# First halves of all heads ahead of second halves in every batch, stacks of two head pairs in the raw weights' room, and the exponential's scale and bias from one VectorE instruction

## The chip, the cores and the metric

The kernel runs on one core of a Trainium2 chip. The metric is the device time of one execution in microseconds, median of several runs. Five engines work side by side, each through its own list of instructions in order: TensorE (PE, with its weight loads listed as PEld), VectorE (DVE), ScalarE (ACT), GpSimd (POOL) and SyncE (SP), which here only issues DMAs.

## What is computed

Four batches of eight attention heads (768 positions, 64 wide) with a hash mask, then a two-layer network over the 3072 tokens:

```
q_bucket, k_bucket = 6 sign bits of q @ proj, k @ proj
scores = where(q_bucket == k_bucket, q @ k.T / 8, -1e9)
attn   = softmax(scores);  x = attn @ v          # x: 3072 x 512
out    = relu(x @ w_in)**2 @ w_out               # w_in 512 x 2048, w_out 2048 x 512
```

## The kernel before, in words

**Units and visits.** Heads are taken in pairs (four pairs, `hp`, to a batch `b`). A visit `(b, hp, half)` handles 384 of the 768 query rows for both heads of a pair: six units of 128 rows, three for each head (`unit`, L720). There are 32 visits and 192 units, numbered from 0 in the code and from 1 in the text. A unit computes 128 x 768 scores in PSUM (`pS`), a row maximum on DVE (the tile `line`), the exponential on ACT (`e`), and then in the later visits two float16 halves of the divided rows (`hl`, ACT and DVE), which one DMA transposes into `aT`. In early "plain" visits (`PLAIN_AV`) the rows stay float32, GpSimd divides them, TensorE transposes them (`pT`) and ACT or DVE copies them to `aT`. `av` (L764) multiplies `aT` with the values into `pA` and splits the result into `xx`.

**Scores and stacks.** In batch 0 the scores are one float32 product of two stacked operands (tiles `A`, `Q`, `L`, `M`; a matmul `pS<-A,L` or `pS<-Q,M`). In batches 1 to 3 they are two float16 products of four stacked operands (`A`, `Q`, `L`, `M`, each half a tile). `prep` (L627) makes a pair's stacks: it loads the pair (`R<-kq`), computes the sign bits (`pd`, `bits`) and their masks (`pc`), in batches 1 to 3 also power-of-two scales (`bounded`, L596), and sends pieces between partitions by DMA. Each of the four tile names has two buffers, so the stacks of two pairs live at a time.

**Weights.** `fetch` (L517) loads a 128 x 512 piece of a weight matrix (`raw`, two buffers), rebuilds float32 values in `f` (seven buffers, helper tiles `top`), and `split` writes two float16 halves to `win` or `wo`. There are 32 such pieces.

**The network.** When all four pairs of a (batch, half) are done, one of eight stages of `moe` (L787) may start. A stage has 16 steps of 12 matmuls `pm<-xx,win` (384 columns) and 9 matmuls `po<-wo,g` (512 columns). The first stage uses `wo` as converted; `align` (L574) then rescales the 16 slices of `wo` for the other stages (`move` at L584, on ACT, DVE or POOL).

**What sets the order.** All instructions are recorded first (`Program.add`), then a planner (`order`, L244) gives each engine its list, from prices per instruction (`cost`), ranks, and `PACE` (L65), which ties the network's 896 groups of three matmuls to units: a group may not start before its unit's scores. `WHOLE = {0: 2}` and L880 set the visits: in batch 0 pairs 0 and 1 whole, then the first halves of pairs 2 and 3, then their second halves; in batches 1 to 3 every pair whole. So in batches 1 to 3 the first half's stage becomes possible one visit before the second half's. `ALTERNATE = 36` (L723) lets every other of the first 36 units put its scores into the PSUM room of `po`; later units share the single `pS`.

**The lines of a unit that change.** After the maximum, two tiny DVE instructions make the scale and the bias that the exponential reads:

```
todo = [("tensor_reduce", (nmx, sS, AX.XY, ALU.max), {"negate": True})]
if len(st) > 1:
    todo += [("tensor_scalar", (scale, nmx, MASK * MASK / 2, factor[st[1][0].rec], ALU.is_lt, ALU.mult), {}),
             ("tensor_scalar", (bias, nmx, scale, 1.0, ALU.mult, ALU.mult), {})]
```

Of the kernel before, what the change touches and what calls it, by code (L numbers as in the profile page):

```python
# [33 lines left out]
MASK = 49152.0  # L34
ASC = float(2.0**14)


BUFS = dict(xx=12, hl=3, raw=2, f=7, e=3, aT=3, g=2, A=2, Q=2, L=2, M=2, RV=2, VV=6)
# [14 lines left out]
PLAIN, PLAIN_TO, ALTERNATE = 4, 8, 36  # L53

PLAIN_AV, DIVIDE = (0, 1, 2, 4, 5), ("pool",)
# [3 lines left out]
WHOLE = {0: 2}  # L59
# [5 lines left out]
PACE = ((25, 0), (64, 120), (193, 680))  # L65
# [58 lines left out]
class Program:  # L124
# [12 lines left out]
    def tile(self, pool, kind, shape, dtype, name, bufs=1, tag=None):  # L137
        line = self.tags.setdefault((id(pool), tag or name), [])
        make = lambda: pool.tile(shape, dtype, name=name, tag=tag or name, bufs=bufs)
        rec = Buffer(kind, int(np.prod(shape[1:])), line[-bufs] if len(line) >= bufs else None, make)  # L140
        line.append(rec)
        rec.line, rec.bufs = line, bufs
        self.n += 1
        return View(rec, self.shadow.dram_tensor(f"{name}_{self.n}", shape, dtype, kind="Internal").ap(), ())

    @staticmethod
    def region(view):
        ap, rec = view.ap, view.rec
        size = lambda dims: 1 + sum(st * (n - 1) for st, n in dims)
        if rec.kind == "dram":  # L150
            return 0, 1, ap.offset, ap.offset + size(ap.ap), 0, 0, 0
        p0, f0 = divmod(ap.offset, rec.row)
        if rec.kind == "psum":
            return 0, 1, 0, 1, 0, 0, 0

        (step, n), inner = ap.ap[1], size(ap.ap[2:])
        block = (step, f0 % step, f0 % step + inner) if n > 1 and f0 % step + inner <= step else (0, 0, 0)
        return (p0, p0 + ap.ap[0][1], f0, f0 + size(ap.ap[1:])) + block
# [32 lines left out]
    def cost(key, name, args, kw):  # L191
# [3 lines left out]
        if name == "chain":  # L195
            t = sum(Program.cost(key, *x)[0] for x in args)
            return t, t
# [245 lines left out]
def lsh_attention_moe(ctx: ExitStack, tc, kq, v, proj2, w_in, w_out, consts, out):  # L443
# [44 lines left out]
    sgn_f = sb([P, 4 * P], F32, "sgn_f", tag="o")  # L488
# [23 lines left out]
    tops = [sb([P, 512, 2], F16, f"top{n}") for n in range(2)]  # L512
    for x in tops:
        dve.memset(x.bitcast(F32), 0.0)
    turn = [0]

    def fetch(src):  # L517

        raw = sb([P, 512, 2], U32, "raw", BUFS["raw"])
# [4 lines left out]
        f = sb([P, 512], F32, "f")  # L524
        dve.scalar_tensor_tensor(f.bitcast(U32), raw[:, :, 0], 13, first.rearrange("p n t -> p (n t)").bitcast(U32), ALU.logical_shift_right, ALU.bitwise_or)
        return f
# [47 lines left out]
    def align():  # L574
# [17 lines left out]
    halved, factor = [], {}  # L592
# [3 lines left out]
    def bounded(Rs):  # L596
# [17 lines left out]
        both = sb([P, 8], F32, "both")  # L614
        size, flip = both[:, 0:4], both[:, 4:8]
        dve.tensor_scalar(size, pn, 2.0**8, 2.0**120, ALU.max, ALU.min)
        dve.tensor_scalar(u32(size), u32(size), 1, 0x7F800000, ALU.logical_shift_right, ALU.bitwise_and)
        dve.tensor_scalar(u32(flip), u32(size), 0x7F800000, 0x7F800000, ALU.bitwise_xor, ALU.bitwise_and)
        found = sb([P, 4], F32, "found", 4)
        own, exact = found[:, 0:2], found[:, 2:4]  # L620
        for n, h in enumerate((T, U)):
            dve.tensor_scalar(own[h], flip[h, 2 * n : 2 * n + 2], 2.0**-51, 1.0, ALU.mult, ALU.mult)
        dve.tensor_scalar(size, size, 2.0**50, 1.0, ALU.mult, ALU.mult)
        dve.scalar_tensor_tensor(exact, size[:, 0:2], SC, size[:, 2:4], ALU.mult, ALU.mult)
        return own, exact

    def prep(b, hp, plain):  # L627
# [19 lines left out]
        if not plain:  # L647
            own, exact = bounded(Rs)
        out = []
        for odd, R in enumerate(Rs):  # L650
# [3 lines left out]
            else:  # L654

                A, Q, L, M = [x[:, n] for x in (sb([P, 2, S], F16, name) for name in ("AL", "QM")[odd]) for n in range(2)]
# [19 lines left out]
            else:  # L676
# [3 lines left out]
                factor[M.rec] = exact[:, odd : odd + 1]  # L680
# [4 lines left out]
    def scale_values(b):  # L685
# [3 lines left out]
        for hp in range(H // 2):  # L689
# [30 lines left out]
    def unit(st, half, i, aT, plain):  # L720
# [9 lines left out]
        line = sb([P, 3], F32, "line", 2)  # L730
        nmx, bias, scale = [line[:, n : n + 1] for n in range(3)]
        todo = [("tensor_reduce", (nmx, sS, AX.XY, ALU.max), {"negate": True})]
        if len(st) > 1:
            todo += [("tensor_scalar", (scale, nmx, MASK * MASK / 2, factor[st[1][0].rec], ALU.is_lt, ALU.mult), {}),
                     ("tensor_scalar", (bias, nmx, scale, 1.0, ALU.mult, ALU.mult), {})]
# [3 lines left out]
        to = {"bias": bias, "scale": scale} if len(st) > 1 else {"bias": nmx}  # L739
# [47 lines left out]
    def moe(n, b, half):  # L787
# [5 lines left out]
        for f in range(NF + 1):  # L793
# [21 lines left out]
            if f > 0:  # L815
# [17 lines left out]
                if n == 0 and m == 3:  # L833
                    acc = sb([P, 3, DM], F32, "acc")
                for t in range(3):
# [8 lines left out]
                    elif last:  # L844
                        o = sb([P, DM], F32, "o", tag="f")

# [31 lines left out]
    for b in range(B):  # L878
        F = WHOLE.get(b, H // 2)
        visits += [(b, hp, half) for hp in range(F) for half in range(2)] + [(b, hp, 0) for hp in range(F, H // 2)] + [(b, hp, 1) for hp in reversed(range(F, H // 2))]  # L880
# [72 lines left out]
```

## Time and profile before

| What | Value |
|---|---|
| Median of 3 runs | 904.04 us (901.77 to 905.07) |
| The profiled execution's own time | 904.71 us |
| Its span, first to last instruction | 902.9 us |
| Mean granted TensorE clock | 0.994 |
| PE busy | 850.8 us, 94% |
| DVE busy | 685.0 us, 76% |
| ACT busy | 666.7 us, 74% |
| POOL busy | 107.7 us, 12% |
| DMA queue of SP, share of 16 engines | 62.1% |

The profile shows one execution. Busy times are sums over the span; a stage of the kernel is looked at through windows of the span. The row maximum of unit 24 starts at 81.1 us, of unit 36 at 126.9, unit 48 at 185.3, unit 72 at 285.5 and unit 192 at 769.8; the stages below are cut just behind the 24th, 72nd and 192nd.

### The profile page before, as it was taken

How to read it: one execution, taken by the hardware profiler on the slowest of the kernel's cores; microseconds unless marked ns; L12 is line 12 of the kernel's file. 1: busy time of each engine (PE TensorE's matmuls, PEld its weight loads, DVE VectorE, ACT ScalarE, POOL GpSimd, SP SyncE). 2: the span in 40 equal slices, each digit the busy share in tenths (PEclk: the TensorE clock that was granted, in tenths of full speed). 3: DMA queues.
4: the chain of work that ended last, by engine and by line, in shares of the span. 5: the costliest groups of instructions: out<-in, count | busy, mean ns of one | idle time of the engine just before them, and what ended most of it. 6: DMA issues, size and time to landing. Idle time of an engine off the chain costs nothing. (4 is left out here: it accounts for less than half of the span.)

```text
span 902.9 us, 14665 instructions
## 1 busy us (share of the span) xinstructions
PE 850.8 (94%) x5095; PEld 449.6 (50%) x5095; DVE 685.0 (76%) x1563; ACT 666.7 (74%) x1217; POOL 107.7 (12%) x158
## 2 busy tenths in 40 slices
PE   8997989998888999799999999999999999999997
PEld 6553544554444555445454555544445555555553
DVE  5899889999999888888888888898879876211111
ACT  4875777998789988888879887888779766533433
POOL 1665554100200000000000000000000000000000
PEclk9998999999999999999999999999999999999999
DMA  7447637689878676868879776777757736400000
GB/s 246 138 152 199 198 111 210 134 169 193 177 157 158 141 139 133 180 131 170 167 124 204 120 150 103 170 148 119 156 112 167 123 53 116 77 1 1 35 1 36
DMA packets 279978, 120.06 MB, mean 133 GB/s; under 512 B 258272, under 2 KB 266080, under 8 KB 279904
## 3 DMA queue, kind: packets, MB, share of 16 engines
q1 hardware_dynamic: 279424, 119.11, 62.1%
q8 instruction: 40, 0.66, 0.3%
q14 instruction: 34, 0.28, 0.1%
q10 hardware_dynamic: 480, 0.01, 0.0%
HBM read 37.30 MB, written 6.29 MB: 48 GB/s over the span
## 5 line engine op out<-in xcount | busy, mean ns | idle before, releaser
L430 PE MATMUL po<-wo,g 128*128 128x512 f16 x1152 | 324.4, 379 | 3.6 <-DVE g L430 1.5
L430 PE MATMUL pm<-xx,win 128*128 128x384 f16 x1536 | 322.6, 326 | 3.9 <-ACT g L430 2.8
L430 ACT ACTIVATE e<-pS,line 128x768 f32<-128x768 f32 x192 | 185.7, 967 | 65.1 <-DVE line L428 56.0
L430 PEld LDWEIGHTS <-win 128*128 128x128 f16 x1536 | 149.3, 98 | 117.1 <-issue 10.8
L428 DVE TENSOR_REDUCE line<-pS 128x1 f32<-128x768 f32 x192 | 182.7, 952 | 29.6 <-PE pS L430 27.7
L430 PEld LDWEIGHTS <-g 128*128 128x128 f16 x1152 | 110.7, 98 | 131.2 <-issue 11.8
L430 DVE SCALAR_TENSOR_TENSOR hl<-e,rv,hl 128x768 f16<-128x768 f32 x162 | 165.4, 1023 | 9.9 <-ACT hl L430 9.7
L430 ACT ACTIVATE hl<-e,rv 128x768 f16<-128x768 f32 x157 | 145.8, 930 | 30.7 <-ACT e L430 15.2
L430 DVE SCALAR_TENSOR_TENSOR g<-g,g 128x384 f16<-128x384 f32 x118 | 65.6, 556 | 107.7 <-ACT g L430 106.2
L430 ACT ACTIVATE g<-g 128x384 f32<-128x384 f32 (+1 forms) x242 | 125.1, 519 | 5.1 <-PE po L430 0.4
L430 ACT ACTIVATE g<-pm 128x384 f32<-128x384 f32 x128 | 61.8, 483 | 76.2 <-PE pm L430 75.8
L423 PE MATMUL pA<-aT,VV 128*64 128x384 f16 x972 | 87.8, 328 | 0.0
L430 POOL TENSOR_SCALAR rv<-sm 128x1 f32<-128x1 f32 x69 | 26.3, 381 | 484.3 <-ACT e L430 483.3
L423 PEld LDWEIGHTS <-VV 128*64 128x64 f16 x972 | 51.1, 110 | 36.3 <-issue 16.2
L430 PE MATMUL pS<-A 128*128 128x384 f16 x144 | 35.0, 324 | 12.4 <-ACT e L430 11.9
L430 PE MATMUL pS<-Q 128*128 128x384 f16 x144 | 35.8, 325 | 7.9 <-ACT e L430 7.3
L430 PE MATMUL pS<-A,L 128*128 128x384 f32 x96 | 39.7, 529 | 2.8 <-ACT e L430 2.7
L430 PE MATMUL pS<-Q,M 128*128 128x384 f32 x96 | 37.0, 502 | 2.9 <-ACT e L430 2.1
L430 DVE TENSOR_SCALAR rv<-sm 128x1 f32<-128x1 f32 x123 | 18.4, 150 | 25.9 <-ACT e L430 25.7
L430 ACT ACTIVATION_READ_ACCUMULATOR e<-pS,line 128x1 f32 x192 | 37.7, 196 | 0.0
L430 PE MATMUL pS<-M 128*128 128x384 f16 x144 | 35.4, 325 | 0.0
L430 PE MATMUL pS<-L 128*128 128x384 f16 x144 | 35.3, 325 | 0.0
(130 smaller groups left out, 844.2 us busy)
## 6 DMA issues: line engine op xcount, KB each, us to landing
R<-kq SPq DMA_DIRECT2D x24, 384.0 KB
raw<-w_in SPq DMA_DIRECT2D x16, 511.8 KB
raw<-w_out SPq DMA_DIRECT2D x16, 511.8 KB
V<-vp SPq DMA_DIRECT2D x16, 384.0 KB
out<-o SPq DMA_DIRECT2D x21, 256.0 KB
aT<-hl SPq DMA_TRANSPOSE x162
A<-A SPq DMA_DIRECT2D x24, 96.0 KB
Q<-Q SPq DMA_DIRECT2D x24, 96.0 KB
```

What stands on the lines that cost most here:

```text
L423: ins = q.engine.matmul(*map(real, args), **kw).ins
L428: issue(q, getattr(q.engine, name)(*map(real, args), **{k: real(x) for k, x in kw.items()}).ins)
L430: ins = getattr(q.engine, o.name)(*map(real, o.args), **{k: real(x) for k, x in o.kw.items()}).ins
```

## The change

What it does:

- `WHOLE` is 0 for every batch: four first halves (pairs 0 to 3), then four second halves, in batches 1 to 3 in the same order of pairs, in batch 0 in reverse. A first half's stage of the network becomes possible after half of a batch.
- One tile `room` of 26,624 bytes per partition takes the place of `raw`, `top` and `f`. In batches 1 to 3, pairs 2 and 3 put their stacks there; pairs 0 and 1 keep the two buffers of `A`, `Q`, `L`, `M`. So four pairs' stacks live through such a batch. In batch 0 they do not: two pairs are made a second time for their second halves (16 executions of `prep` become 18).
- Plain visits are 0 to 3 in place of 0, 1, 2, 4, 5; `PACE` starts at unit 12 and reaches group 800 at the end in place of 680; `ALTERNATE` falls from 36 to 24.
- `bounded` scales one head's two operands so that the product needs no factor. `unit` then makes scale and bias at once, as a `[P, 2]` result of one `scalar_tensor_tensor` on a line that holds 1.0 and the negated maximum.
- `align` is bound to POOL. Outputs use `acc` in place of buffers of `f`. The planner's price of a chain has 120 ns more per link.

```
-WHOLE = {0: 2}
+WHOLE = {0: 0, 1: 0, 2: 0, 3: 0}
-PACE = ((25, 0), (64, 120), (193, 680))
+PACE = ((12, 0), (36, 60), (193, 800))
-PLAIN, PLAIN_TO, ALTERNATE = 4, 8, 36
+PLAIN, PLAIN_TO, ALTERNATE = 4, 8, 24
-PLAIN_AV, DIVIDE = (0, 1, 2, 4, 5), ("pool",)
+PLAIN_AV, DIVIDE = (0, 1, 2, 3), ("pool",)
+ALIGN_ON = ("pool",)
...
+    room = sb([P, ROOM // 4], F32, "room")
+    place = lambda at, size, dtype: room[:, at // 4 : (at + size) // 4].bitcast(dtype)
...
-            move(x, x, rel[:, n // 4 : n // 4 + 1])
+            move(x, x, rel[:, n // 4 : n // 4 + 1], engines=tuple(getattr(pr, k) for k in ALIGN_ON))
...
+                if b and hp >= 2:
+                    A, Q, L, M = [place(12288 * (hp - 2) + 6144 * odd + 1536 * n, 1536, F16) for n in range(4)]
+                else:
...
-            todo += [("tensor_scalar", (scale, nmx, MASK * MASK / 2, factor[st[1][0].rec], ALU.is_lt, ALU.mult), {}),
-                     ("tensor_scalar", (bias, nmx, scale, 1.0, ALU.mult, ALU.mult), {})]
+            pair = sb([P, 2], F32, "pair", 2)
+            todo += [("scalar_tensor_tensor", (pair, nmx.broadcast_to([P, 2]), MASK * MASK / 2, line, ALU.is_lt, ALU.mult), {})]
+            to = {"scale": pair[:, 0:1], "bias": pair[:, 1:2]}
...
-    for b ... + [(b, hp, 1) for hp in reversed(range(F, H // 2))]
+    for b ... + [(b, hp, 1) for hp in (reversed(range(F, H // 2)) if F or not b else range(H // 2))]
```

The order of the built programs gives, on TensorE, these counts of matmuls up to the scores of a unit (before / after):

| Up to | pm | po | pA f16 | pA f32 | pT | pd | pc |
|---|---|---|---|---|---|---|---|
| unit 24 | 0 / 0 | 0 / 0 | 0 / 0 | 36 / 36 | 108 / 123 | 12 / 16 | 8 / 16 |
| unit 72 | 240 / 349 | 160 / 248 | 216 / 252 | 60 / 48 | 180 / 144 | 32 / 44 | 30 / 41 |
| unit 192 | 1164 / 1308 | 864 / 971 | 936 / 960 | 60 / 48 | 180 / 144 | 64 / 72 | 64 / 72 |
| the end | 1536 / 1536 | 1152 / 1152 | 972 / 1008 | 60 / 48 | 180 / 144 | 64 / 72 | 64 / 72 |

On TensorE before, between the scores of units 31 and 36, the list holds float32 scores and transposes, with single matmuls `pt` of the weights' norms:

```order
L430 MATMUL pS_1339<-A,L 128x384
L430 MATMUL pT<-unit_f,e 128x128 x4
L430 MATMUL pS_1339<-A,L 128x384
L430 MATMUL pT<-unit_f,e 128x128 x2
L430 MATMUL pS<-A,L 128x384
L430 MATMUL pT<-unit_f,e 128x128 x3
```

and in the changed kernel, at the same units, the scores stand between the network's matmuls:

```order
L434 LDWEIGHTS win
L434 MATMUL pm<-xx,win 128x384
L434 MATMUL pS<-A,L 128x384 x2
L434 LDWEIGHTS win
L434 MATMUL pm<-xx,win 128x384
```

The first stage of the network has moved from units 37 and on to units 25 and on, and the plain transposes of these units are gone.

On VectorE before, a unit near the 100th has the maximum, the two tiny instructions, and then other work:

```order
L428 TENSOR_REDUCE line<-pS 128x1
L428 TENSOR_SCALAR line<-line,found 128x1
L428 TENSOR_SCALAR line<-line 128x1
L430 SCALAR_TENSOR_TENSOR hl<-e,rv,hl 128x768
L430 SCALAR_TENSOR_TENSOR g<-g_4823,g 128x384
```

and now, at the same place:

```order
L432 TENSOR_REDUCE line_74<-pS 128x1
L432 SCALAR_TENSOR_TENSOR pair<-line_74 128x2
L434 SCALAR_TENSOR_TENSOR hl<-e,rv,hl 128x768
L434 SCALAR_TENSOR_TENSOR g<-g_5059,g 128x384
```

One instruction has gone from between the maximum and what follows.

On GpSimd before, three slices of `wo` were rescaled there (eight were on ACT, five on DVE):

```order
L430 TENSOR_SCALAR rv<-sm 128x1
L430 TENSOR_SCALAR wo<-wo,rel 128x2x512 x3
L430 TENSOR_SCALAR rv<-sm 128x1 x5
```

and now all sixteen are:

```order
L434 TENSOR_SCALAR wo<-wo,rel 128x2x512 x2
L434 TENSOR_SCALAR rv<-sm 128x1
L434 TENSOR_SCALAR wo<-wo,rel 128x2x512 x4
L434 TENSOR_SCALAR rv<-sm 128x1
L434 TENSOR_SCALAR wo<-wo,rel 128x2x512 x10
```

Thirteen rescalings have moved to GpSimd's list, some of the unit's `rv` behind them. VectorE's last conversion of a weight piece stands at unit 36 now, at unit 48 before.

More of the change, by code (lines that the diff above doesn't have):

```diff
@@ L139, in tile @@
         make = lambda: pool.tile(shape, dtype, name=name, tag=tag or name, bufs=bufs)
-        rec = Buffer(kind, int(np.prod(shape[1:])), line[-bufs] if len(line) >= bufs else None, make)
+        rec = Buffer(kind, int(np.prod(shape[1:])) * mybir.dt.size(dtype), line[-bufs] if len(line) >= bufs else None, make)
         line.append(rec)
@@ L151, in region @@
             return 0, 1, ap.offset, ap.offset + size(ap.ap), 0, 0, 0
-        p0, f0 = divmod(ap.offset, rec.row)
         if rec.kind == "psum":
             return 0, 1, 0, 1, 0, 0, 0
-        (step, n), inner = ap.ap[1], size(ap.ap[2:])
-        block = (step, f0 % step, f0 % step + inner) if n > 1 and f0 % step + inner <= step else (0, 0, 0)
-        return (p0, p0 + ap.ap[0][1], f0, f0 + size(ap.ap[1:])) + block
+        k = mybir.dt.size(view.dtype)
+        p0, f0 = divmod(ap.offset * k, rec.row)
+        (step, n), inner = ap.ap[1], size(ap.ap[2:]) * k
+        step *= k
+        block = (step, f0 % step, f0 % step + inner) if n > 1 and step and f0 % step + inner <= step else (0, 0, 0)
+        return (p0, p0 + ap.ap[0][1], f0, f0 + (size(ap.ap[1:]) - 1) * k + k) + block
     def add(self, *ways):
@@ L195, in cost @@
         if name == "chain":
-            t = sum(Program.cost(key, *x)[0] for x in args)
+            t = sum(Program.cost(key, *x)[0] for x in args) + 120 * (len(args) - 1)
             return t, t
@@ L511, in lsh_attention_moe @@
     wo = sb([P, 2, NF, DM], F16, "wo")
[L512 removed]
+    room = sb([P, ROOM // 4], F32, "room")
+    place = lambda at, size, dtype: room[:, at // 4 : (at + size) // 4].bitcast(dtype)
+    tops = [place(8192 + 2048 * n, 2048, F16).rearrange("p (n t) -> p n t", t=2) for n in range(2)]
     for x in tops:
[L514 to L515 removed]
+        dve.memset(x.rearrange("p n t -> p (n t)").bitcast(F32), 0.0)
+    turn, turned = [0], [0]
     def fetch(src):
[L519 removed]
+        raw = place(turn[0] % 2 * 4096, 4096, U32).rearrange("p (n t) -> p n t", t=2)
         send(raw.rearrange("p n t -> p (n t)").bitcast(U16)[:, 0:2047], src.bitcast(U16)[:, 1:2048])
@@ L590, in matmuls @@
         pr.add((pe, "matmuls", [(a, {"start": start, "stop": stop}) for a in args], {}))
-    halved, factor = [], {}
+    halved = []
+    lines = [sb([P, 2], F32, f"line{n}") for n in range(2)]
+    for x in lines:
+        dve.memset(x, 1.0)
     few = sb([P, 4], BF16, "few")
@@ L647, in prep @@
         if not plain:
-            own, exact = bounded(Rs)
+            own = bounded(Rs)
         out = []
@@ L688, in scale_values @@
         tops = sb([P, H // 2], F32, "vtop", 2)
-        for hp in range(H // 2):
+        for hp in range(H // 2) if b else reversed(range(H // 2)):
             pr.rank = r0 + LOADS * hp
@@ L832, in moe @@
                     back = unscaled(b, m // 4)
-                if n == 0 and m == 3:
+                if last and (n or m == 3):
                     acc = sb([P, 3, DM], F32, "acc")
@@ L879, in lsh_attention_moe @@
         F = WHOLE.get(b, H // 2)
-        visits += [(b, hp, half) for hp in range(F) for half in range(2)] + [(b, hp, 0) for hp in range(F, H // 2)] + [(b, hp, 1) for hp in reversed(range(F, H // 2))]
+        visits += [(b, hp, half) for hp in range(F) for half in range(2)] + [(b, hp, 0) for hp in range(F, H // 2)] + [(b, hp, 1) for hp in (reversed(range(F, H // 2)) if F or not b else range(H // 2))]
     kept, kept_v = {}, {}
```

42 lines of the change are left out of this document (23 added, 19 removed).

## Prediction

> **What bounds the kernel now.** First the page's busy shares:
>
> ```profile
> span 902.9 us, 14665 instructions
> PE 850.8 (94%) x5095; PEld 449.6 (50%) x5095; DVE 685.0 (76%) x1563; ACT 666.7 (74%) x1217; POOL 107.7 (12%) x158
> ```
>
> TensorE is idle for 52 us only. If the change takes no matmul away, it can win little more than these 52 us. Where they lie is read from windows, cut behind the 24th, 36th, 48th, 72nd and 192nd row maximum (columns: width, then busy time of PE, PEld, DVE, ACT, POOL, granted clock, DMA share, GB/s):
>
> ```profile
> 0.00:82.10 82.10, 75.81 (x449) 45.59 (x450) 66.87 (x144) 54.83 (x115) 42.05 (x57) 1.00 0.59 180
> 82.10:126.90 44.80, 37.03 (x179) 19.83 (x179) 39.58 (x84) 30.86 (x61) 21.21 (x31) 0.89 0.58 176
> 126.90:185.30 58.40, 54.43 (x283) 28.18 (x282) 54.98 (x121) 49.25 (x93) 21.25 (x29) 1.00 0.69 166
> 185.30:286.50 101.20, 89.08 (x563) 46.06 (x562) 96.37 (x228) 87.79 (x150) 9.76 (x14) 1.00 0.85 168
> 286.50:770.80 484.30, 468.72 (x2938) 244.47 (x2937) 405.54 (x951) 390.79 (x698) 13.39 (x28) 1.00 0.73 140
> 770.80:902.90 132.10, 125.72 (x691) 65.41 (x688) 21.68 (x40) 53.17 (x104) 0.00 (x0) 1.00 0.07 22
> ```
>
> ```profile
> L428 DVE TENSOR_REDUCE line<-pS x192: 930/951/960, 15.7 to 769.8; 128x1 f32<-128x768 f32 x192
> ```
>
> The last row gives the maxima's first and last start. I call row one of the windows stage 1, rows two to four together stage 2 (units 25 to 72, 204.4 us), row five stage 3, row six stage 4. PE's idle time is 6.3, 23.9, 15.6 and 6.4 us. In stage 2 PE works 180.5 us and DVE 190.9 of the 204.4: there VectorE is the bound (weights are converted, and the first units with float16 stacks begin), and TensorE lacks work that it could do. In stage 3 PE is busy 97%, DVE 84%, ACT 81%. Stage 4 is the network alone.
>
> What TensorE and the row's chain wait for, over the span:
>
> ```profile
> ACT e L430 <- DVE line L428: 56.0, 71, 2.5
> ...
> PE pS L430 <- ACT e L430: 24.1, 31, 2.8
> ```
>
> From unit 37 on there is one score buffer, so the next scores wait for the exponential, and that waits for `line`. Inside, on DVE:
>
> ```profile
> 190.59 0.94 DVE L428 TENSOR_REDUCE line<-pS 128x1 f32<-128x768 f32 x1
> 191.57 0.21 DVE L428 TENSOR_SCALAR line<-line,found 128x1 f32<-128x1 f32 x1
> 191.82 0.21 DVE L428 TENSOR_SCALAR line<-line 128x1 f32<-128x1 f32 x1
> 191.95 1.01 DVE L430 SCALAR_TENSOR_TENSOR hl<-e,rv,hl 128x768 f16<-128x768 f32 x1
> ```
>
> Each dependent link costs 0.25 us (191.82 less 191.57), which is more than its 0.21.
>
> **Part 1: matmuls moved.** Prices come from the chain of waits in stage 4 and from the groups by shape:
>
> ```profile
> 777.35 0.86 PE po L430 x4
> 778.22 1.14 PE pm L430 x7
> 781.25 0.86 PE po L430 x4
> ```
>
> ```profile
> L423 PE MATMUL pA<-aT,VV 128*64 128x384 f16 x972 | 87.8, 328 | 0.0
> ...
> L430 DVE SCALAR_TENSOR_TENSOR g<-g,g 128x384 f16<-128x384 f32 x118 | 65.6, 556 | 107.7 <-ACT g L430 106.2 <-PE pn L430 0.5
> ...
> L430 PE MATMUL pT<-unit_f,e 128*128 128x128 f32 x180 | 27.4, 276 | 2.2 <-ACT aT L430 1.3 <-POOL e L430 0.5 <-DVE cst L430 0.4
> ...
> L430 PE MATMUL pc<-bits,sgn 128*128 128x384 bf16 x64 | 21.3, 333 | 8.6 <-DVE L L430 4.7 <-DVE M L430 2.5 <-DVE norm L430 0.9
> ...
> L423 PE MATMUL pA<-aT,V 128*64 128x384 f32 x120 | 20.5, 490 | 0.3 <-ACT aT L430 0.3
> ...
> L423 PE MATMUL pd<-R,pj 128*32 128x384 f32 x96 | 10.7, 498 | 0.0
> ```
>
> A step of the network (12 `pm`, 9 `po`) takes 3.90 us (781.25 less 777.35); by columns that is 0.162 us a `pm` and 0.216 a `po`. The others, busy over count: `pA` 0.090, `pT` 0.152, `pc` 0.33, and, with two records to a float32 matmul, `pA` f32 0.34 and `pd` 0.22.
>
> With the counts of the change section, up to unit 24: 15 `pT` 2.3, 4 `pd` 0.9, 8 `pc` 2.7: +5.9 us. Up to unit 72: 109 `pm` 17.7, 88 `po` 19.0, 36 `pA` 3.3, 12 `pA` f32 -4.1, 36 `pT` -5.5, 12 `pd` 2.7, 11 `pc` 3.7: +36.8. Up to unit 192: 144 `pm` 23.3, 107 `po` 23.1, 24 `pA` 2.2, -4.1, -5.5, 8 `pd` 1.8, 8 `pc` 2.7: +43.5. At the end: 3.3 - 4.1 - 5.5 + 1.8 + 2.7 = -1.8. So TensorE's work by stage becomes 75.8 + 5.9 = 81.7; 180.5 + 30.9 = 211.4; 468.7 + 6.7 = 475.4; 125.7 - 45.3 = 80.4; together 848.9, as much as before. The gain can come only from idle time, 31 us of work having gone into the stage where PE had 24 us to spare. The second making of two pairs is in these sums; of the other three batches none is made again, since `bounded` stands twelve times in both orders.
>
> **Part 2: VectorE and ScalarE.** In stage 2 DVE gets 9 more `hl` (float16 visits from unit 25 on; 1.01 us each, row in part 3), 9.2 us; 7 more of the network's `g`, 3.9; one more `bounded`, and in each of its five there six more tiny instructions of at most a link, 0 to 7.5, taken as 4. It loses 24 links of 0.25, 6 us, and five rescalings of 0.48, 2.4. That is about +9: 200 us of work. ACT gets nine more `hl` of 0.93 and the moved network's squares and loses eight rescalings of 1.15; I take it as 168 to 178. In stage 3 DVE loses 120 links, 30 us, and gets 7 x 6 x 0.25 = 10 back in `bounded`: 386 us.
>
> The price of the new instruction is not in the trace. The two old ones take 0.38 us together until the next one starts (191.95 less 191.57); the one new one takes at least the second's 0.13 and at most the 0.38, where nothing is saved. I take 0.13, as it differs from the second old one only in being twice as wide. If nothing is saved, DVE has 206 and 416 us, still under PE; I price that at 4 us, the part of the idle time that the shorter chain is to win in stage 3. The rest of the shortening lies under PE's work, since PE waited for the exponential only 31 times.
>
> DMA: six more transposes, two more plain pairs loaded, all by unit 72, where the engines' share was 0.85 at most. SP's list is in order, and what is queued behind them are weight loads and the next stacks. I take nothing for it, and up to 3 us if a load comes late. Writing stacks into `room` waits for the last conversion. That stands at unit 36 on DVE, and the first scores from `room` are unit 61's, 24 units later: hidden.
>
> **Part 3: `align` on POOL.** The rows of the rescalings and of `hl`, with shortest, median and longest time:
>
> ```profile
> L430 ACT ACTIVATE wo<-wo,rel x8: 1137/1150/1157, 258.9 to 273.6; 128x1024 f16<-128x1024 f16 x8
> L430 DVE TENSOR_SCALAR wo<-wo,rel x5: 469/477/479, 262.1 to 268.1; 128x1024 f16<-128x1024 f16 x5
> ...
> L430 POOL TENSOR_SCALAR wo<-wo,rel x3: 1117/1118/1817, 245.0 to 247.1; 128x1024 f16<-128x1024 f16 x3
> ```
>
> ```profile
> L430 DVE SCALAR_TENSOR_TENSOR hl<-e,rv,hl x162: 998/1009/1584, 74.0 to 775.3; 128x768 f16<-128x768 f32 x162
> L430 SPq DMA_TRANSPOSE aT<-hl x162: 1273/1439/2463, 75.1 to 776.4; - x162
> L430 ACT ACTIVATE hl<-e,rv x157: 917/934/949, 76.0 to 774.4; 128x768 f16<-128x768 f32 x157
> ```
>
> Sixteen take 16 x 1.12 = 18 us on POOL, or 29 at the longest. A slice is needed every 3.90 us of the next stage, so POOL keeps ahead; behind it wait only some `rv`, which can also stand on DVE. It takes 2.4 us from DVE and 9.2 from ACT. The longest POOL row is 0.70 us over its median, the longest `hl` 0.58 over its own: two engines seem to get into each other's way at times, and I set that at 2 us, within the idle time below. The Trainium skill ("SBUF — State Buffer", section "Who interferes with whom") says that a VectorE instruction with two SBUF inputs and a GpSimd instruction that reads SBUF exclude each other for a whole instruction; the two longest rows agree, and by that rule the thirteen moved slices speak against the change.
>
> **The clock.** One stretch of stage 2:
>
> ```profile
> 85.00:90.00 5.00, 2.99 (x6) 1.56 (x6) 4.77 (x11) 2.09 (x3) 1.74 (x3) 0.50 0.64 171
> ```
>
> Here PE starved and ran at half speed. With the network's matmuls beside units 25 and on, such a hole closes; The 2.99 us at half speed are 1.5 us of work; I count 0 for it, and 1.5 us at the low end. The Trainium skill ("TensorE: Matmul & The Clock Gate", Part 1) puts the halved clock down to an idle window and lifts it after a few microseconds of work; by that rule the 1.5 us would be won in full, 885.5 in place of 887.
>
> **The sum.** Stage 1: 81.7 + 6.3 idle = 88.0. Stage 2: 211.4 + 12 = 223.4; the 12 are chosen, between 7 (stage 3's share of idle time, 3.2%) and the old 23.9, nearer to stage 3, because PE is now the longest there (211 against 200), but three engines are over 80%. Stage 3: 475.4 + 12 = 487.4, of 15.6 about a quarter won by the shorter chain. Stage 4: 80.4 + 6.4 = 86.8; in the order 36 `pm` and 29 `po`, 12 us, stand behind the last scores ahead of the last `pA`. Before, the last maximum began at 769.8 and the last transpose was issued at 776.4 and took 1.4 us, so 8 us go by there, and 4 are left for its landing; if it lands later, each microsecond counts. Span 885.6; the profiled execution took 1.8 us more than its span (904.71 and 902.9), so 887.4, put at 887, against 904.71 of that execution and a median of 904.04. About 0.5% can be told from no change: under 899.5 is faster, over 908.6 slower.
>
> **Rivals.**
>
> *The idle time stays.* Stage 2 keeps 23.9 and stage 3 15.6, since DVE, ACT and PE all near their limits wait for each other: 887 + 11.9 + 3.6 = 902.5. For it: in the last part of stage 2 before, PE lost 12.1 of 101.2 us although the network was there. Against it: DVE was then 95% busy, and will be 90% (200 of 223.4). Chance 0.13.
>
> *The single score buffer binds, slower.* From unit 25 on there is one `pS`, twelve units earlier, while DVE still converts weights. If each of units 25 to 48 finds one more DVE instruction of `hl`'s 1.01 us ahead of its maximum, PE, in order, stands 24 x 1.01 = 24 us: 911. It decides when the units' period passes what PE has to do, 223.4 / 48 = 4.65 us. For it: units 25 to 36 had two buffers and DVE was busy 39.58 of 44.80. Against it: units 37 to 48 had one, at 4.87 us each, and PE was 93% busy. Chance 0.15.
>
> *GpSimd and VectorE in each other's way.* Thirteen POOL rescalings each hold DVE up for 0.58 to 1.12 us, on the path: 7.5 to 14.6 us, 894 to 902, middle 898. Against it: one of three POOL rows only was long. Chance 0.05.
>
> *Nearly all idle time goes.* Stage 2 at 7, stage 3 at 5 (1%), the clock's 1.5: 887 - 5 - 7 - 1.5 = 873.5. Chance 0.07.
>
> **How the numbers follow.** The forecast has the remaining 0.60. Faster: 0.60 + 0.07 + 0.05 = 0.72; same 0.13; slower 0.15. The range goes from 870, under the best case, to 906, over the rival in which idle time stays; the slower one is left out.
>
> **What would show it.** Right: the 72nd maximum near 310 us (88.0 + 223.4), PE at 94% or more in units 25 to 72, one link of 0.2 to 0.3 us behind each maximum, some 87 us behind the last. Wrong: `PE pS <- ACT e` grown over 24 us and units 25 to 48 longer than 4.65 us each (slower rival); long POOL and `hl` rows during the rescalings (the two in each other's way); PE idle as before in stage 2.

## The result, and the profile after

The changed kernel takes 892.49 us (median of 4 runs, 891.39 to 893.71), the kernel before 904.26 (4 runs, 901.77 to 905.07): a ratio of 0.9875, interval 0.9851 to 0.9898, or 11.8 us less. The profiled execution took 893.71 us, with a granted clock of 0.988 over the span.

The page's busy shares of the changed kernel:

```profile
span 891.9 us, 14603 instructions
PE 845.0 (95%) x5079; PEld 448.0 (50%) x5083; DVE 671.6 (75%) x1482; ACT 670.3 (75%) x1223; POOL 114.8 (13%) x153
```

TensorE's idle time is 46.9 us (891.9 less 845.0), where it was 52.1. Windows of the changed kernel, cut behind the 24th, 72nd and 192nd maximum (columns as before: width, busy PE, PEld, DVE, ACT, POOL, clock, DMA share, GB/s):

```profile
0.00:88.70 88.70, 79.90 (x470) 48.00 (x475) 72.14 (x161) 62.15 (x127) 45.05 (x65) 1.00 0.56 174
88.70:330.60 241.90, 215.77 (x1199) 108.32 (x1198) 205.47 (x440) 181.21 (x324) 62.64 (x71) 0.96 0.72 163
330.60:805.50 474.90, 469.35 (x2964) 250.22 (x2963) 379.02 (x855) 393.10 (x707) 7.13 (x17) 1.00 0.74 141
805.50:891.90 86.40, 80.01 (x452) 41.47 (x449) 15.00 (x28) 33.88 (x66) 0.00 (x0) 0.98 0.12 33
```

The width of a row less its PE time is the idle time: 8.8, 26.1, 5.5 and 6.4 us, against 6.3, 23.9, 15.6 and 6.4 before. One start time given ahead of the prediction is wrong: in the kernel before, the 24th maximum starts at 81.98 us (81.1 is the 23rd), so the cut at 82.1 lies inside it. Cut behind it, stage 2 of the kernel before is 203.5 us long with 23.0 us of idle time, and stage 1 has 7.1:

```profile
82.95:286.50 203.55, 180.54 (x1021) 94.08 (x1021) 190.08 (x429) 167.10 (x302) 52.21 (x73) 0.97 0.74 169
```

So stage 2 kept its idle time and has 3 us more; stage 3 lost two thirds of its own. The waits of the changed kernel (total, times, longest):

```profile
ACT e L434 <- DVE pair L432: 43.2, 53, 3.6
...
PE pS L434 <- ACT e L434: 14.4, 15, 3.0
```

Before, ScalarE waited 56.0 us for the scale and bias and TensorE 24.1 us for the exponential. The chain inside, on VectorE in stage 3 of the changed kernel (start, duration):

```profile
470.32 0.95 DVE L432 TENSOR_REDUCE line<-pS 128x1 f32<-128x768 f32 x1
471.31 0.16 DVE L432 SCALAR_TENSOR_TENSOR pair<-line 128x2 f32<-128x2 f32 x1
471.40 1.02 DVE L434 SCALAR_TENSOR_TENSOR hl<-e,rv,hl 128x768 f16<-128x768 f32 x1
```

The next instruction starts 0.09 us behind the start of `pair` (471.40 less 471.31). The two old links took 0.38, so a unit saves 0.29 us of VectorE's list. The exponential gains as much: in stage 3 it starts 0.29 us behind the end of the maximum (median of the 120 units), where it was 0.59.

**Where stage 2 loses its time.** The longest stretch without a maximum is between units 36 and 37. TensorE of the changed kernel there (start, duration; in brackets the idle time ahead and its releaser), and the loads on SP's queue that this stretch begins with:

```profile
142.95 1.56 PE L434 MATMUL pS<-Q,M 128*128 128x384 f32 x4
...
160.83 0.38 PE L434 MATMUL pt<-sq,ones 128*128 128x512 bf16 x1 [3.13 <-ACT sq L434]
162.08 0.85 PE L427 MATMUL pd<-A,pj 128*32 128x384 f32 x2 [0.88 <-DVE norm L434]
...
165.59 0.50 PE L434 MATMUL pc<-bits,sgn 128*128 128x384 bf16 x1
...
170.27 0.32 PE L434 MATMUL pc<-bits,sgn 128*128 128x384 bf16 x1 [0.77 <-DVE L L434]
...
172.01 1.56 PE L434 MATMUL pS<-A,L 128*128 128x384 f32 x4 [0.33 <-ACT L L434]
```

```profile
146.25 0.34 SPq L434 DMA_DIRECT2D room<-w_out  x1
146.64 0.90 SPq L434 DMA_DIRECT2D Q<-kq  x2
```

Unit 37 belongs to pair 1 of batch 0, which is made a second time, into the buffers of pair 2. Pair 2's second half (units 31 to 36) reads these until its last score (`pS<-Q,M`, 142.95 to 144.51). The load stands in SP's list behind that of a weight piece and starts at 146.64, and sign bits (`pd`, 162.08), masks (`pc`, 165.59) and pieces follow one after another, until scores start at 172.01. Not all of this stop is the pair's own: `pt` belongs to a piece of `w_out` and stands ahead of the pair's `pd` in TensorE's list. It waited 3.13 us for that piece's `sq`, and `pd` another 0.88 for its `norm`. The window from unit 36's maximum to unit 37's, and one in the later part of stage 2, in which GpSimd rescales `wo`:

```profile
147.20:174.60 27.40, 20.80 (x111) 8.59 (x110) 22.79 (x49) 15.53 (x27) 3.55 (x4) 0.88 0.65 177
...
245.00:262.00 17.00, 11.37 (x53) 5.66 (x52) 15.21 (x21) 9.77 (x18) 16.83 (x14) 0.80 0.49 108
```

TensorE is idle for 6.6 and 5.6 us there, and it works at a mean clock of 0.88 and 0.80. The other 13.9 of stage 2's 26.1 us lie elsewhere in shorter pieces, the longest of them 3.01 us. In the second window GpSimd is busy for 16.83 of 17.0 us, and VectorE's instructions grow. The tile rows (shortest, median, longest) and three instructions of VectorE in that window:

```profile
L434 POOL TENSOR_SCALAR wo<-wo,rel x16: 1117/1126/1947, 226.1 to 262.4; 128x1024 f16<-128x1024 f16 x16
...
L434 DVE SCALAR_TENSOR_TENSOR hl<-e,rv,hl x168: 992/1018/1867, 96.0 to 808.7; 128x768 f16<-128x768 f32 x168
...
L432 DVE SCALAR_TENSOR_TENSOR pair<-line x144: 160/160/954, 228.9 to 805.5; 128x2 f32<-128x2 f32 x144
```

```profile
254.10 0.71 DVE L432 SCALAR_TENSOR_TENSOR pair<-line 128x2 f32<-128x2 f32 x1
...
255.21 1.87 DVE L434 SCALAR_TENSOR_TENSOR hl<-e,rv,hl 128x768 f16<-128x768 f32 x1
...
260.01 1.47 DVE L434 SCALAR_TENSOR_TENSOR g<-g,g 128x384 f16<-128x384 f32 x1
```

`pair` takes 0.71 us in place of 0.16 (and once 0.95, at 262.62), one `hl` 1.87 in place of 1.02, one `g` 1.47 in place of 0.56.

### The profile page after: what moved, and what is told of

Same layout as the page of the kernel before. It is cut to its first block, busy times and chain, and to the rows that moved or that the text cites. A ratio compares the mean times of both kernels' runs of the same rounds, so it can differ in the third digit from the quotient of the medians.

```text
span 891.9 us, 14603 instructions
## 1 busy us (share of the span) xinstructions
PE 845.0 (95%) x5079; PEld 448.0 (50%) x5083; DVE 671.6 (75%) x1482; ACT 670.3 (75%) x1223; POOL 114.8 (13%) x153
## 5 line engine op out<-in xcount | busy, mean ns | idle before, releaser
L434 PE MATMUL po<-wo,g 128*128 128x512 f16 x1152 | 317.4, 379 | 3.6 <-ACT g L434 1.5
L434 DVE SCALAR_TENSOR_TENSOR hl<-e,rv,hl 128x768 f16<-128x768 f32 x168 | 172.4, 1027 | 17.9 <-ACT hl L434 17.4
L434 ACT ACTIVATE e<-pS,pair 128x768 f32<-128x768 f32 x144 | 142.2, 987 | 54.6 <-DVE pair L432 43.2
L434 ACT ACTIVATE hl<-e,rv 128x768 f16<-128x768 f32 x166 | 153.8, 929 | 27.3 <-ACT e L434 16.3
L434 ACT ACTIVATE g<-g 128x384 f16<-128x384 f32 (+1 forms) x251 | 130.1, 519 | 5.8 <-PE po L434 1.4
L434 DVE SCALAR_TENSOR_TENSOR g<-g,g 128x384 f16<-128x384 f32 x118 | 66.5, 564 | 81.3 <-ACT g L434 80.4
L434 PE MATMUL pS<-room 128*128 128x384 f16 x288 | 59.8, 326 | 1.9 <-ACT hl L434 1.3
L434 ACT ACTIVATE e<-pS,line 128x768 f32<-128x768 f32 x48 | 43.2, 900 | 8.0 <-DVE line L432 8.0
L434 PEld LDWEIGHTS <-room 128*128 128x128 f16 x288 | 27.0, 98 | 27.5 <-issue 8.0
L434 DVE RECIPROCAL rv<-rv 128x1 f32<-128x1 f32 x192 | 30.7, 161 | 6.3 <-POOL rv L434 1.0
L432 DVE SCALAR_TENSOR_TENSOR pair<-line 128x2 f32<-128x2 f32 x144 | 25.9, 180 | 5.1
```

Source lines behind the costliest of these rows:

```text
L432: issue(q, getattr(q.engine, name)(*map(real, args), **{k: real(x) for k, x in kw.items()}).ins)
L434: ins = getattr(q.engine, o.name)(*map(real, o.args), **{k: real(x) for k, x in o.kw.items()}).ins
```

## The experiments

Two questions are open after the two traces: why stage 2 keeps its idle time, and why stage 3 wins 9.4 us (484.3 to 474.9) where the prediction's link was worth 4. For stage 2, theory A says that the two stretches have each a cause of its own (the second making of a pair; the rescalings on GpSimd) and can be mended one by one; its rival B, that VectorE is saturated there and what is mended turns up elsewhere. For stage 3, theory D says that the chain's length on the chip makes the difference; its rival C, that it is the planner's lists, which were built for too short a chain before and no longer are, its price now having 120 ns more a link.

Most edits let the planner lay out every list anew. Three runs keep the lists as they are and change only what is issued at the places in question; the text says "lists fixed" of them. All ratios are to the kernel before, which was timed again beside each group of runs; its median lay between 902.75 and 904.26 us, so where two runs differ by a few microseconds the ratios compare better than the times. A range in us is that of the runs, one behind a ratio its 95% interval.

### align_spread: rescalings on three engines again

```
-ALIGN_ON = ("pool",)
+ALIGN_ON = ("act", "dve", "pool")
```

> The changed kernel with the rescalings of wo free for ACT, DVE and POOL again, as before the change. Theory A (the thirteen rescalings on POOL and VectorE's two-input instructions hold each other up, in the changed kernel from 248.9 to 262.5 us): hl, g and the new two-wide instruction are at their short times again during the rescalings, TensorE loses neither its 5.4 us of idle time nor its 3.4 us at half speed there, and the time falls by 5 to 9 us, to 883 to 887 us. Rival B (VectorE is simply full in units 25 to 72, and the slices put back on ACT and DVE, 8 x 1.15 and 5 x 0.48 us, take what is won): 891 to 896 us.

Measured: 895.68 us (894.81 to 896.39), ratio 0.9915 (0.9889 to 0.9941). B's number and not A's: 3 us slower than the changed kernel. But the planner laid out all lists anew, and stage 3 was 485.1 us long in place of 474.9, so this run could not tell what the slices alone do. `slices_only` asks that again.

### second_halves_2301: pair 2's second half first, then 3, 0, 1

```
-    ... + [(b, hp, 1) for hp in (reversed(range(F, H // 2)) if F or not b else range(H // 2))]
+    ... + [(b, hp, 1) for hp in (reversed(range(F, H // 2)) if F else range(H // 2) if b else (2, 3, 0, 1))]
```

A pair made again now finds its buffers free one visit earlier.

> The changed kernel with batch 0's second halves in the order of pairs 2, 3, 0, 1 in place of 3, 2, 1, 0. Two pairs are still made a second time, but each takes the buffers of a pair whose visit ended one visit earlier. Theory A (the scores of unit 37 wait for a pair that can be made again only when unit 36 has read the old one: 27.4 us from maximum to maximum there, against some 5): that gap falls under 8 us, the hole in TensorE's work between 147 and 175 us closes (6.6 us idle, 3.3 us at half speed, and what hangs on it), and the time falls by 7 to 14 us, to 878 to 886 us. Rival B (units 25 to 72 are bound by VectorE's sum of work, the gap is only where it shows): 889 to 894 us.

Measured: 892.87 us (891.26 to 894.21), ratio 0.9884 (0.9856 to 0.9912): as the changed kernel. The same stretch, from unit 36's maximum to unit 37's, in this kernel:

```profile
150.70:170.80 20.10, 19.42 (x122) 9.71 (x121) 17.74 (x36) 11.60 (x21) 2.82 (x3) 1.00 0.58 155
```

The two maxima still lie 20.1 us apart, which is not the gap under 8 us that was expected, but TensorE now works for 19.42 of them, at full clock. So the hole hangs on the order of the second halves, as A has it. The weight pieces' `pt` come without a wait there too, so the run does not tell the pair's own wait from that behind the piece. The 72nd maximum came at 318.8 us in place of 329.5. These 10.7 us did not reach the end: stage 3 took 483.1 us in place of 474.9. For the end, B's number is the right one, although the time was lost in another stage than the one B speaks of.

### both_mended: both edits

```
+ALIGN_ON = ("act", "dve", "pool")
...
+    ... else (2, 3, 0, 1))]
```

> Both edits together, rescalings spread over three engines and batch 0's second halves in the order 2, 3, 0, 1. Theory A, two separate causes: the gains add, 12 to 22 us, 870 to 881 us, and TensorE's idle time in units 25 to 72 falls from 26 to about 14 us. Rival B, one saturated engine: 888 to 896 us.

Measured: 888.08 us (886.7 to 890.91), ratio 0.9836 (0.9799 to 0.9872), 4.4 us under the changed kernel; their runs do not overlap, but the intervals of their ratios do. Stage 2's idle time was 20.0 us. The time lies where B has it (888 to 896); A wanted 870 to 881, and 14 us of idle time. Stage 3 was again longer, 484.8 us.

### two_links: scale and bias by two dependent instructions

```
-            todo += [("scalar_tensor_tensor", (pair, nmx.broadcast_to([P, 2]), MASK * MASK / 2, line, ALU.is_lt, ALU.mult), {})]
+            todo += [("tensor_scalar", (pair[:, 0:1], nmx, MASK * MASK / 2, 1.0, ALU.is_lt, ALU.mult), {}),
+                     ("tensor_scalar", (pair[:, 1:2], nmx, pair[:, 0:1], 1.0, ALU.mult, ALU.mult), {})]
```

> The changed kernel with scale and bias made by two dependent VectorE instructions again, as before the change, all else as in the changed kernel (the planner lays the lists out anew with the longer chain). If the shorter chain is what cut TensorE's idle time in units 73 to 192 from 15.6 to 5.5 us: idle time there back at 12 to 16 us and the time 6 to 11 us longer, 898 to 904 us. If the more even spread of the network's matmuls did it, and the chain lies under TensorE's work: 891 to 895 us, idle time there 5 to 8 us, only VectorE's busy time 25 to 36 us higher.

Measured: 888.93 us (885.81 to 893.77), ratio 0.9846 (0.9803 to 0.9888). A longer chain, and yet no slower; it lies under both numbers that were expected. Its windows for stages 2 and 3:

```profile
86.30:315.20 228.90, 208.93 (x1181) 106.70 (x1180) 205.33 (x450) 180.04 (x326) 64.90 (x79) 0.98 0.77 171
315.20:798.60 483.40, 473.67 (x2987) 252.26 (x2985) 398.24 (x968) 395.52 (x708) 18.57 (x31) 1.00 0.71 139
```

Stage 3 did get 8.5 us longer (483.4 against 474.9), while stage 2 got 13.0 us shorter (228.9 against 241.9). That comes by another layout and not by its links, of which it has more. Wherever the planner may lay out anew, a stage can move by this much for no reason that lies in the edit. So the next three keep the lists.

### slices_only: thirteen slices back on ACT and DVE, lists fixed

At the place where GpSimd's list has the 16 slices, the emitter hands eight to ACT and five to DVE.

```
+            if q.key == "pool" and o.name == "tensor_scalar" and o.args[0].rec is o.args[1].rec and len(o.args[0].shape) == 3:
+                self.slices = getattr(self, "slices", 0) + 1
+                q = {"a": self.act, "d": self.dve, "p": self.pool}["pppadadadadadaaa"[self.slices - 1]]
...
```

> The changed kernel with every engine's list as the planner left it, but for thirteen of the sixteen rescalings of wo, which are taken from POOL's list to ACT's (8) and VectorE's (5) at their place in the planned order. Nothing else moves, unlike in the run that let the planner choose again. Theory A (POOL's rescalings and VectorE's two-input instructions block each other): pair, hl and g at their short times throughout, the half clock near 255 us gone, and 5 to 9 us less than the changed kernel, 883.5 to 887.5 us. Rival B (the slices cost ACT and VectorE what they cost on POOL): 890 to 895 us.

Measured: 894.63 us (893.22 to 895.58), ratio 0.9905 (0.9886 to 0.9923). VectorE's `hl` over the span, and the stretch of the rescalings, in this kernel:

```profile
L440 DVE SCALAR_TENSOR_TENSOR hl<-e,rv,hl x168: 1000/1018/1021, 96.8 to 807.8; 128x768 f16<-128x768 f32 x168
```

```profile
245.00:262.00 17.00, 10.93 (x48) 5.44 (x48) 11.77 (x23) 13.92 (x23) 0.19 (x1) 0.80 0.49 94
```

The long rows are gone: the longest `hl` is 1.02 us, where it was 1.87. But TensorE is idle for 6.1 us of the 17, where it was 5.6, and the time is B's. The rescalings on GpSimd do lengthen VectorE's instructions, and yet it wins nothing to move them away. In the changed kernel TensorE's list there reads:

```profile
248.24 2.11 PE L434 MATMUL pm<-xx,win 128*128 128x384 f16 x12
252.26 0.48 PE L434 MATMUL pS<-A 128*128 128x384 f16 x2 [1.91 <-ACT e L434]
...
256.06 0.80 PE L434 MATMUL pS<-A 128*128 128x384 f16 x2 [2.99 <-ACT e L434]
...
257.30 3.64 PE L434 MATMUL pm<-xx,win 128*128 128x384 f16 x12
```

and in `slices_only` the same two waits of TensorE, and ScalarE ahead of the first:

```profile
251.97 0.48 PE L440 MATMUL pS<-A 128*128 128x384 f16 x2 [2.82 <-ACT e L440]
...
255.22 0.80 PE L440 MATMUL pS<-A 128*128 128x384 f16 x2 [2.44 <-ACT e L440]
```

```profile
249.81 1.13 ACT L438 ACTIVATE wo<-wo,rel 128x1024 f16<-128x1024 f16 x1
250.85 0.97 ACT L440 ACTIVATE e<-pS,pair 128x768 f32<-128x768 f32 x1
```

The second wait shrank from 2.99 to 2.44 us, with VectorE's rows short again. The first grew from 1.91 to 2.82: a slice now stands on ScalarE right ahead of the exponential. So one delay was traded for another. Until `wo` is rescaled no `po` can be in the list, and from 248 us on only scores and some `pm` are; two units' scores stand one behind the other, and the single score buffer makes each wait for the exponential. That reading rests on the two lists and the releasers; no run put other work there, and none left the rescalings out, so how deep the hole would be without them is open.

### links_only: two dependent links in place of the one, lists fixed

```
+                    if name == "scalar_tensor_tensor":
+                        pair, nmx = args[0], args[3][:, 1:2]
+                        issue(q, q.engine.tensor_scalar(real(pair[:, 0:1]), real(nmx), MASK * MASK / 2, 1.0, ALU.is_lt, ALU.mult).ins)
+                        issue(q, q.engine.tensor_scalar(real(pair[:, 1:2]), real(nmx), real(pair[:, 0:1]), 1.0, ALU.mult, ALU.mult).ins)
+                        continue
```

> The changed kernel with every engine's list as planned, but with scale and bias made by two dependent VectorE instructions at the place of the one. Nothing else moves. If the chain's length sets TensorE's idle time in units 73 to 192: 6 to 11 us longer than the changed kernel, 898 to 904 us. If the chain lies under TensorE's work: 891 to 895 us, with VectorE's busy time 25 to 30 us up. Bound from the new instruction's row (0.18 against twice 0.21 us): no more than 144 x 0.25 = 36 us.

Measured: 907.85 us (906.98 to 909.65), ratio 1.0053 (1.0035 to 1.0070). The second link alone, in the same lists, costs 15.4 us over the changed kernel and undoes the whole gain. Stage 3 of this kernel, and then its waits in that window:

```profile
331.50:820.00 488.50, 476.15 (x2964) 249.77 (x2963) 400.03 (x976) 394.94 (x707) 8.17 (x17) 1.00 0.72 137
```

```profile
ACT e L439 <- DVE pair L435: 45.7, 64, 3.6
```

The same waits in stage 3 of the changed kernel:

```profile
ACT e L434 <- DVE pair L432: 33.3, 43, 3.6
```

Stage 3 is 13.6 us longer (488.5 against 474.9), 0.11 us for each of its 120 units. The exponential starts 0.24 us later here (0.53 us behind the end of the maximum, median, against 0.29). Half of the 13.6 us shows as idle time of TensorE (12.4 against 5.5 us). The other half, 6.8 us, stands in its busy time: 476.15 against 469.35 for the same 2964 matmuls, which in both kernels have the same mean duration to 2 ns for each kind. A record lasts 326 ns and the next `pm` starts 0.16 us behind it; so when the flow stops, the last record covers part of the stop. A busy sum hides such stops. The stops can be counted from the starts instead: for each of the nine commonest kinds of matmul, take what the time to the next start has above its median. This gives 28.0 us in the changed kernel and 41.0 in this one: 13.0 more, nearly the whole difference. What TensorE's waits name is far less. The changed kernel and this one in stage 3:

```profile
PE pS L434 <- ACT e L434: 2.2, 3, 1.5
```

```profile
PE pS L439 <- ACT e L439: 6.6, 12, 1.9
```

Two things limit this run. The lists were laid out for the shorter chain, so theory C expects a loss here as D does. And the second link gives VectorE 21 us more work in the stage (400.03 against 379.02) besides its delay; the run does not part the two.

### before_slices_on_pool: the kernel before with all 16 slices on GpSimd, lists fixed

```
+            if o.name in ("tensor_scalar", "activation") and isinstance(o.args[1], View) and o.args[0].rec is o.args[1].rec and ...:
+                issue(self.pool, self.pool.engine.tensor_scalar(real(o.args[0]), real(o.args[1]), x, 1.0, ALU.mult, ALU.mult).ins)
```

> The kernel before with every engine's list as planned, but for the thirteen rescalings of wo that stood on ACT (8) and VectorE (5), which go to POOL at their place in the planned order. Theory A: VectorE's two-input instructions grow long from 245 to 275 us, TensorE loses time there, and the kernel takes 4 to 9 us longer, 907 to 913 us. Rival B: 901 to 906 us, since ACT and VectorE get 11 us of work less.

Measured: 906.24 us (904.42 to 912.75), ratio 1.0042 (1.0023 to 1.0060), about 4 us slower. `hl` was up to 1.87 us long here too. Together with `slices_only`, where putting them back cost 2.1 us, which is not clear of noise (the intervals of the ratios overlap): moving the slices either way won nothing.

### old_visits: the change without its order of visits

```
-WHOLE = {0: 0, 1: 0, 2: 0, 3: 0}
+WHOLE = {0: 2}
-PACE = ((12, 0), (36, 60), (193, 800))
+PACE = ((25, 0), (64, 120), (193, 680))
-PLAIN, PLAIN_TO, ALTERNATE = 4, 8, 24
+PLAIN, PLAIN_TO, ALTERNATE = 4, 8, 36
-PLAIN_AV, DIVIDE = (0, 1, 2, 3), ("pool",)
+PLAIN_AV, DIVIDE = (0, 1, 2, 4, 5), ("pool",)
-ALIGN_ON = ("pool",)
+ALIGN_ON = ("act", "dve", "pool")
...
```

The pace, the plain visits, `ALTERNATE` and the engines of the rescalings go back with the visits. The one tile `room`, the new `bounded`, the single link and its price stay.

> The changed kernel with the order of visits, the pace, the plain visits, the alternating score room and the engines of the rescalings as before the change; room, the new scaling and the one instruction for scale and bias stay. If the order of visits is where the gain comes from: 899 to 905 us. If the shorter chain and the lighter VectorE are: 890 to 896 us.

Measured: 885.62 us (883.3 to 886.7), ratio 0.9796 (0.9772 to 0.9821). It is the fastest of all, 6.9 us under the changed kernel, and below both numbers that were expected. Its stages 2 to 4:

```profile
86.30:280.80 194.50, 178.49 (x1026) 93.54 (x1025) 181.03 (x412) 162.68 (x295) 58.51 (x78) 1.00 0.80 172
280.80:752.90 472.10, 463.42 (x2931) 244.95 (x2929) 381.07 (x866) 388.93 (x698) 12.65 (x27) 1.00 0.74 145
752.90:884.90 132.00, 125.57 (x690) 65.33 (x687) 21.28 (x39) 53.01 (x104) 0.00 (x0) 1.00 0.07 22
```

Against before, stage 1 is 3.3 us longer (86.3 against 82.95), stage 2 9.0 us shorter (194.5 of 203.5), stage 3 12.2 us (472.1 of 484.3), and the tail is as it was. Against the changed kernel, idle time in stage 2 is 16.0 in place of 26.1 us and the clock is full. In these layouts the new order of visits, with the pace, the plain visits and the rescalings that were set with it, brings nothing that the rest of the change does not bring without it.

### before_price_only, no_price, old_visits_no_price: the planner's 120 ns

The first adds the price to the kernel before, the second takes it from the changed kernel, the third from `old_visits`.

```
-            t = sum(Program.cost(key, *x)[0] for x in args) + 120 * (len(args) - 1)
+            t = sum(Program.cost(key, *x)[0] for x in args)
```

> The kernel before with one edit: the planner's price of a chain has 120 ns more per link, as in the changed kernel. No instruction is added or taken away; only the lists are laid out anew. Theory C (the lists were built for a chain shorter than the chip's, so that each unit's exponential comes later than planned and the in-order lists stand; the change mends this by a shorter chain and by the price): 886 to 895 us. Rival D (what counts is the chain's length on the chip): 901 to 906 us.

> The changed kernel without the 120 ns per link in the planner's price. Theory C: the chain is again priced too short, by 0.12 us a unit, and 896 to 904 us result. Rival D: 890 to 895 us.

> The run with the old order of visits and one link (885.6 us), without the 120 ns per link in the price. Theory C: 890 to 898 us. Rival D: 883 to 889 us.

Measured: 900.91 us (898.6 to 902.8), ratio 0.9966 (0.9950 to 0.9981); 901.59 (898.01 to 903.8), ratio 0.9971 (0.9958 to 0.9984); 897.69 (894.48 to 898.97), ratio 0.9922 (0.9903 to 0.9941). Without the price the changed kernel keeps 2.7 us of its 11.8; the price is worth 9.1 us there, 12.1 with the old visits, and about 3 on the kernel before. C's price helps each time, less on the kernel before than C has it. D's shorter chain may help without the price too: `old_visits_no_price` is about 7 us under before, but it differs from that kernel by `room`, `bounded` and its layout as well.

### old_visits_two_links: the two links of two_links in old_visits

The edit is that of `two_links`, made in `old_visits`, with the price.

> The run with the old order of visits (885.6 us), with two dependent links on the chip and in the planner's price. Theory C (a chain that is priced right costs little, as with the new order of visits, 888.9 us with two links against 892.5 with one): 883 to 890 us. Rival D (144 units wait 0.25 us longer, of which 13.5 us were lost with the lists fixed): 895 to 902 us. If this is near 886 us, the gain of the changed kernel over the one before owes nothing to the one instruction for scale and bias by itself.

Measured: 915.27 us (912.27 to 918.07), ratio 1.0120 (1.0100 to 1.0140). Here the second link costs 29.7 us, where in `two_links` it seemed to win 3.6. C had 883 to 890 us and D 895 to 902: neither. The medians side by side, in us:

| Chain, and its price | Visits as before | New visits |
|---|---|---|
| one link, 120 ns priced | 885.6 (`old_visits`) | 892.5 (the change) |
| one link, not priced | 897.7 | 901.6 |
| two links, 120 ns priced | 915.3 | 888.9 (`two_links`) |
| two links, lists of the change | - | 907.9 (`links_only`) |

The first two rows differ by the price alone, in the same direction in both columns. The third does not follow the columns: the two values lie 26 us apart, and what the planner's layout does there is more than what is asked.

## Why the prediction was right or wrong

**The total** came out 5.5 us above the forecast, since two errors of the forecast nearly cancelled: stage 2 took 18.5 us more than its 223.4, stage 3 12.5 us less than its 487.4. That is luck. The forecast wins most of its time in stage 2, where network matmuls were to fill 12 of 23.9 us of idle time; 26.1 us stayed idle. Stage 3 won 10 us of idle time where 4 were forecast. And `old_visits`, which leaves these matmuls where they were, is faster.

**TensorE's work** by stage was right to 6 us: 79.9, 215.8, 469.4 and 80.0 against 81.7, 211.4, 475.4 and 80.4. Stage 2's excess holds work at half speed; stage 3's lack is probably stops that the busy sum before had counted as work, as it does in `links_only`. VectorE had 205.5 and 379.0 us in stages 2 and 3 against 200 and 386, and ScalarE 181.2 in stage 2, over its 168 to 178.

**Stage 1 and the tail** were right: 88.7 and 86.4 us against 88.0 and 86.8. The matmuls behind the last scores cover the last unit's chain.

**The link.** The step that failed is "I price that at 4 us", with "the rest of the shortening lies under PE's work, since PE waited for the exponential only 31 times". With lists fixed, a second link costs 15.4 us, 13.6 of them in stage 3. The saving itself, 0.25 us a unit, was nearly right (0.29). Wrong was to read the limit from TensorE's waits, 24.1 us in 31 pieces: ScalarE waited for VectorE 71 times, and each list is in order, so a later exponential moves every list behind it, and part of that lands inside TensorE's busy sum: of the 13.6 us of `links_only` only 4.4 show as TensorE's wait for the exponential. The prediction also left out the 120 ns of the planner's price, which stands in the change and, with lists laid out anew, is worth 9.1 us. What the shorter chain alone won over the kernel before is not shown: no run takes a link out of that kernel's lists.

**Stage 2's idle time.** The step that failed is the chosen 12, "nearer to stage 3, because PE is now the longest there". PE is the longest, 215.8 against 205.5 us of VectorE, and 26.1 us of idle time stay. A stage's sums say nothing of a wait inside it. The second making of two pairs was "in these sums", as work; what it cost was a stop of the units, 27.4 us from maximum to maximum, with TensorE idle for 6.6 us and at 0.88 of the clock. "I take nothing" for the DMA missed one part of this: the pair's load may not start before the last score of the visit ahead (144.51), and started at 146.64. Another part is the weight piece ahead of the pair in TensorE's list, 4.0 of the 6.6 us. `second_halves_2301` closed the hole, so that it hangs on the order of the second halves is shown; the share of each wait is not. Of the other 19.5 us, 5.6 lie beside the rescalings and 13.9 in short pieces that no experiment took up. Stage 3 gave back what it won (8.2 of 10.7 us), and why is open.

**The clock** was counted at 0 or as a gain of 1.5 us. It turned out a small loss: the mean clock was 0.96 in stage 2, where before it was 0.89 for 44.8 us and full for the other 159.6. The granted clock was halved in three stretches, 17.1 us together:

```profile
161.41:168.24 6.83, 6.16 (x35) 2.45 (x37) 5.63 (x19) 3.13 (x5) 0.00 (x0) 0.50 0.06 24
226.26:229.68 3.42, 3.42 (x12) 1.48 (x11) 3.39 (x6) 2.18 (x4) 2.74 (x2) 0.50 0.98 187
253.57:260.40 6.83, 4.34 (x14) 2.02 (x14) 6.30 (x8) 3.78 (x7) 6.83 (x6) 0.50 0.72 133
```

The changed kernel's list in `slices_only` has 12 `pm` in 2.11 us, and in 3.64 behind an idle time of 2.99. The Trainium skill ("TensorE: Matmul & The Clock Gate", Part 1) explains a halved clock by an idle window, of about 3.4 us. The rows agree in part: each stretch comes with a stop of over 2.9 us, but the last begins at 253.57, half a microsecond into the idle time of 2.99, with four matmuls of scores between that and an idle time of 1.91. Ahead of it TensorE was not idle for that long. The holes of before had gone, as forecast, and new ones came.

**The rescalings on GpSimd.** The rows that this rival named came: `hl` of 1.87 us, `pair` of 0.71. The Trainium skill's rule ("SBUF — State Buffer", section "Who interferes with whom") agrees with the rows: a VectorE instruction with two SBUF inputs waits while a GpSimd instruction reads SBUF, here for up to 0.91 us beside rescalings of 1.12 (`g`, 0.56 to 1.47). The rival's price, 7.5 to 14.6 us, is not there as a net cost: taking thirteen slices away won nothing (`slices_only`). But the slices cost something on ScalarE and VectorE too, so what the blocking alone costs, and whether the 2 us of the sum were right, is not shown.

**The rivals.** "The idle time stays" was right for stage 2 (26.1 us) and wrong for stage 3 (5.5). The slower rival named two signs. One came: units 25 to 48 took 135.4 us (87.64 to 223.0), 5.6 each, over its 4.65. The other did not: TensorE's wait for the exponential fell to 14.4 us. In units 25 to 48 TensorE waited for the exponential for 2.3 us only, so it was not the score buffer that held these units in the main, but the stop at unit 37; the buffer does show behind them, with 9.3 us up to the 72nd maximum. The signs named for the forecast were mixed: the tail and the link as said, but the 72nd maximum at 329.5 us, not near 310, and PE at 89% in units 25 to 72, not 94%.

**What stays open.** How much of any re-planned kernel's time is its layout. Moves of 10 to 13 us of a stage came with edits that give no reason for them (stage 3 in `align_spread`, stage 2 in `two_links`). The cost of a second link is shown with lists fixed, for lists that were laid out without it; the effect of the price and of the visits only with new layouts, the price three times with one sign, that of the visits once at 6.9 us and once, without the price, at 3.9, both times against the new order. An order of visits is itself the list, so it could not be tried with lists fixed.

## What to carry to other kernels

Where engines take their lists in order and one waits for a short chain in each unit, do not cost the chain by the waits that the longest engine shows. Here 0.24 us more in each of 120 units cost 0.11 us a unit, in lists laid out for the shorter chain; the waits of that engine named a third of it. Price each dependent link in a planner at what the trace shows: the price helped in all three pairs of runs here. And credit an edit with a gain only when it was tried in fixed lists, for a new layout moves as much. When a tile is made a second time, ask first who still reads the buffer that it goes into, and what stands ahead of it in each list.

## What the runs showed of the hardware

A result on 128 x 2 elements costs about what one on 128 x 1 does: `pair` took 0.160 us, and the next, independent instruction started 0.09 us behind its start; of the two links in `links_only` the first took 0.153 and the second, which reads the first's result as a scalar, 0.214.

A GpSimd rescaling can stretch a VectorE instruction with two SBUF inputs by up to 0.91 us (`g`, 0.56 to 1.47; `hl`, 1.02 to 1.87), and a tiny one as well (`pair`, 0.16 to 0.95).

A stop of TensorE cost time behind it as well: around the idle time of 2.99 us the granted clock was 0.50 from 253.57 to 260.40, and the 12 `pm` there took 3.64 us in place of 2.11, half of the hole once more.
